# Decode attention and MLP: the projection of 24 heads is placed between score pieces, and one V multiplication is cut into portions

## The chip, the cores and the metric

The kernel runs on one core of a Trainium2 chip. The metric is the device time of one execution in microseconds (us), the median of several runs. Profiled numbers come from one execution recorded by the hardware profiler. In the profile PE is TensorE (PEld its weight loads), DVE is VectorE, ACT is ScalarE, POOL is GpSimd, and SP is SyncE, which here does nothing but issue DMAs.

## The reference

One decode step of a pre-norm transformer block with a KV cache: 4 sequences (B), one new token each (Sq = 1), width D = 640, 32 heads of 128, 4096 cached keys, and an MLP of width F = 1728 with the Mish activation. All inputs are bfloat16.

```
ln = layernorm(x)
q  = (ln @ wq)                          # 4 x 32 heads x 128
s  = q . k_cache * Dh**-0.5             # per sequence and head: 4096 scores
o  = softmax(s) @ v_cache
h  = x + o.reshape(B, Sq, H*Dh) @ wo
m  = layernorm(h) @ w1 + b1
h2 = h + (m * tanh(softplus(m))) @ w2   # output
```

Each of the K and V caches is 4 x 32 x 4096 x 128 bfloat16, 134 MB. Every element of them is read once.

## The kernel before

**Octets.** The 128 pairs of sequence and head are worked off in 16 groups of 8, called octets here (`NU = 16`). In an octet each pair owns 16 partitions, each partition holds 256 keys (`R = 256`), and K and V of an octet are 8 MB each. The first 14 octets (`NL`) go through one loop on PE (L631); the last two, `U = 14` (the last but one) and `L = 15` (the last), are written out after the loop. They hold the last head rows of two sequences each.

**Scores.** K comes in two halves, `kt[0]` and `kt[1]`, of 128 keys per partition (`RK = 128`), 4 MB each. DVE multiplies K by q in place, a quarter-half at a time (`dve_scores`, L508), four products for a half. PE sums each product over a part of the head width by 8 matmuls against an identity held in the array; such a block of 8 is a *piece* (`pe_pieces`, L428 to L444), and an octet has 8 of them. Each piece waits for its product on the semaphore `to_pe`. Two pieces fill one of two PSUM banks, which DVE then reduces to scores (L494).

**Softmax.** `softmax` (DVE, ACT) and `pe_softmax` (PE) work together: DVE takes row maxima, PE turns them by a small matmul (`tr_row`), DVE reduces, PE spreads the result (`nb_ps`), ACT takes the exponential, DVE masks the weights into a tile `e` of 8 columns per key (L555), and PE sums the rows (`l_ps`). For octet L, `e2[1]` is laid into `kt[1]`, whose scores are done by then.

**V.** `pv_moving` (L464) multiplies rows of V with `e`, four keys per matmul, V moving, into one PSUM bank `p_ps`: 64 matmuls for an octet. ACT copies the bank out (`act_copy`), PE adds its blocks into `ot_b` (`add_blocks`), DVE divides by the sums (`normalise`). There is one V buffer, `v_sb`.

**Projection.** `regroup` turns the normalised outputs of up to six groups of 4 heads into `o4` (PE, then a copy by ACT); `project(hq)` (L658) multiplies one group of 4 heads by `wo`: 20 matmuls of 4 columns, accumulated in `yT_b`. There are 8 such groups (`HQ`); the first 6 (`QA`, 24 heads) are complete after the loop.

**Load queue.** All big loads are issued in program order by SP, each behind explicit waits (`after(sp, ...)`) that protect the buffer it overwrites; one late wait holds back all loads behind it. After the loop the order is: the first half of U's V (L679); the first half of L's K, behind U's fourth piece (L697); the second half of L's K, behind U's last piece (L699); the second half of U's V (L701); the first half of L's V, behind the multiplication of the first half of U's V (L707); the second half of L's V in three steps of a quarter, an eighth and an eighth, behind the multiplication of the second half of U's V (L716); then w1 and w2 into `kt[0]` (L725 to L733).

**PE's order after the loop.** `regroup` of the 24 heads; 14 small matmuls that turn the bias b1, which DVE copies to `b1T` (L688, L689); `project` of the six groups (L691); the pieces of U, its softmax matmuls; V rows 0 to 128 of U (`pv_a`, L706); the pieces of L, its softmax matmuls; V rows 128 to 256 of U (`pv_b`, L714); U's `add_blocks`; V rows 0 to 128 of L; `regroup` and `project` of the seventh group; V rows 128 to 192 of L, then `add_blocks`, then rows 192 to 256 straight into `ot_b` (L754); the eighth group's projection; second layernorm and MLP. The waits on PE, DVE and ACT are all written out by hand, and each engine works strictly in program order.

Of the kernel before, what the change touches and what calls it, by code (L numbers as in the profile page):

```python
# [30 lines left out]
def kernel(  # L31
# [31 lines left out]
    te, ve, ac, po, sp = nc.tensor, nc.vector, nc.scalar, nc.gpsimd, nc.sync  # L63
# [8 lines left out]
    R = Sk // PH  # L72
    KT = 2
    RK = R // KT
# [9 lines left out]
    NL = NU - 2  # L84
# [8 lines left out]
    C2 = F // 128  # L93
    FREM = F - C2 * 128
    FC = C2 + 1
    W1_PARTS = ((0, 3), (3, DC))
    QA = HQ - 2
# [3 lines left out]
    def sb(name, shape, dtype=FP32):  # L101
# [15 lines left out]
    b1_row = sb("b1_row", [1, F], BF16)  # L117
    ident = sb("ident", [128, 128], BF16)
# [17 lines left out]
    e2 = [  # L136
        sb("e2_0", [128, R, R8], BF16)[:, :, :],
        kt[1][:, :, :].rearrange("p r d -> p (r d)")[:, 0 : R * R8].rearrange("p (r i) -> p r i", i=R8),
    ]
# [5 lines left out]
    rs8 = sb("rs8", [128, R8])  # L145
# [4 lines left out]
    b1T = sb("b1T", [128, FC])  # L150
# [5 lines left out]
    s_b = [bank("s0"), bank("s1")]  # L156
# [6 lines left out]
    y2_b = bank("y2_b")  # L163


    pe = Events(tc, "pe")
    dve = Events(tc, "dve")
# [16 lines left out]
    def after(engine, *events):  # L184
        for sem, n in events:
            if seen.get((engine.engine, id(sem)), 0) < n:
                seen[engine.engine, id(sem)] = n
                engine.wait_ge(sem, n)
# [5 lines left out]
    def take(sem, k=1):  # L194
        te.wait_ge(sem, k)
        te.sem_inc(sem, -k)  # L196

    def mm(out_, lhsT, rhs, start=True, stop=True):
        return te.matmul(out_, lhsT=lhsT, rhs=rhs, start=start, stop=stop)  # L199
# [41 lines left out]
    k_ready, v_ready = {}, {}  # L241
# [22 lines left out]
    def load_v(u, r0=0, r1=R):  # L264
        for part, view in keys_in(u, A_v_cache, r0, r1):
            dma = sp.dma_start(out=v_sb[part, r0:r1, :], in_=view)
            if u < NL:
                dma.then_inc(v_in, 16)
            else:
                name = f"v{u}_{r0}"  # L270
                if name not in loads:
                    loads[name] = Events(tc, name)
                v_ready[u, r0] = loads[name].by(dma, 16)
# [8 lines left out]
            out=ident[:, :],  # L282
            in_=ident[:, :],
# [23 lines left out]
    for s in range(n_sub):  # L307
# [11 lines left out]
            out=ln1[:, :],  # L319
# [13 lines left out]
    for src, dst in ((ln1_v, tp[0]), (x_v, tp[1])):  # L333
        for c in range(DC):
            i = mm(dst[:, c, :], src[:, c, :], ident[0:N, 0:N])
# [7 lines left out]
    for b in range(N):  # L343
        ve.tensor_copy(
            out=sel_o[:, b, :, :],
            in_=id32[:, b, :].unsqueeze(2).to_broadcast([N * R8, R8, PH]),
        )
    for k in range(NB):
        ev = ve.tensor_copy(
            out=sel_b[:, k, :, :, :],  # L350
            in_=ident[0 : N * R8, 0 : N * R8]
# [6 lines left out]
    with nc.allow_low_precision("ones and zeros"):  # L358
        ve.tensor_reduce(
            out=mask[0][:, :],  # L360
            in_=ident[:, :].rearrange("p (i x) -> p i x", i=R8),
# [4 lines left out]
            out=mask[1][:, :].rearrange("p (b q) -> p b q", b=NB),  # L366
            in_=ident[:, :].rearrange("p (q x b) -> p b q x", q=G, b=NB),
# [5 lines left out]
            out=pick[:, :],  # L373
            in_=ident_f[:, :].rearrange("p (t i) -> p i t", t=T),
# [42 lines left out]
    for k in range(NB):  # L417
        i = mm(
            qb[:, k, :],
            sel_b[:, k, :, :, :].rearrange("r q x b -> r (q x b)"),  # L420
            q_st[:, HO - 1, :],
        )
# [2 lines left out]
    qb_ok[N] = act.by(ac.copy(out=qbs[:, NL:NU, :], in_=qb))  # L425


    def pe_pieces():  # L428
        te.ldweights(ident[:, :])
        done = []  # L430
        for k in range(KT):
            for part in range(NP):
                for j in range(NQ):
                    take(to_pe.sem)
                    for d in range(j * DQ, (j + 1) * DQ, W):
                        i = mm_held(
                            s_ps[part],
                            ident[:, :],
                            kt[k][:, part * RP : (part + 1) * RP, d : d + W],
                            start=(d == 0),  # L440
                            stop=(d == Dh - W),
                        )
                    done.append(pe.by(i))
        return done  # L444

    tr_row = small[0:1, 0:128]
# [1 line left out]
    l_ps = small[:, 136 : 136 + R8]  # L448
    ot_ps = [ot_b[:, i * R8 : (i + 1) * R8] for i in range(2)]

    def pe_softmax():
        done = []
        for o, lhsT, rhs in (
            (tr_row, pm, ident_f),
            (nb_ps, nscale, mx),
            (l_ps, ones_f, rs8),
        ):
            take(to_pe.sem)
            done.append(pe.by(mm(o, lhsT[:, :], rhs[:, :])))

        take(to_pe.sem)
        return done

    def pv_moving(e, r0, r1, last):  # L464
        for r in range(r0, r1, J):
            c0 = 128 // T * (r // J % T)
            i = mm(
                p_ps[c0 : c0 + J * R8, :],
                e[:, r : r + J, :].rearrange("p j i -> p (j i)"),
                v_sb[:, r : r + J, :].rearrange("p j d -> p (j d)"),  # L470
                start=(r < J * T),
                stop=(r >= last - J * T),
            )
        return i
# [44 lines left out]
    def softmax(u, done, e):  # L519
        to_pe.by(ve.tensor_reduce(out=pm[:, :], in_=s_sb[:, :], axis=AX.X, op=ALU.max))  # L520
        after(ve, done[0])
        if rows(u) is None:
            m = mask[0]
            o, i = mx[:, :], tr_row.rearrange("o (i x) -> o i x", i=R8)
        else:
            m = mask[1]
            o = mx[:, :].rearrange("o (b q) -> o b q", b=NB)
            i = tr_row.rearrange("o (q x b) -> o b q x", q=G, b=NB)
        to_pe.by(ve.tensor_reduce(out=o, in_=i, axis=AX.X, op=ALU.max))  # L529

        after(ve, done[1])
        then(ve, dve, ve.tensor_tensor(out=nb8[:, :], in0=nb_ps, in1=m[:, :], op=ALU.mult))  # L532
        after(ac, dve.by(ve.tensor_reduce(out=nbs[:, :], in_=nb8[:, :], axis=AX.X, op=ALU.add)))  # L533
        exp_ok = act.by(
            ac.activation(  # L535
                out=e1[:, :],
                in_=s_sb[:, :],
                func=ACT.Exp,
                bias=nbs[:, :],
                scale=SCALE,  # L540
                accum_out=rs[:, u : u + 1],
            )
        )

        after(ve, exp_ok)
        to_pe.by(
            ve.tensor_tensor(  # L547
                out=rs8[:, :],
                in0=rs[:, u : u + 1].to_broadcast([128, R8]),
                in1=m[:, :],  # L550
                op=ALU.mult,
            )
        )
        to_pe.by(
            ve.tensor_tensor(  # L555
                out=e,
                in0=e1[:, :].unsqueeze(2).to_broadcast([128, R, R8]),
                in1=m[:, :].unsqueeze(1).to_broadcast([128, R, R8]),
                op=ALU.mult,
            )  # L560
        )
        after(ve, done[2])
        return dve.by(ve.reciprocal(out=rl[u % 2][:, :], in_=l_ps))

    def act_copy(done):
        after(ac, done)
        p_out.by(ac.copy(out=p_sb[:, :], in_=p_ps[:, :]))  # L567
# [29 lines left out]
    wo_in = b1_in = None  # L597
    wo = Events(tc, "ld_wo")
    for u in range(NL):
# [6 lines left out]
        if N <= u < 2 * N:  # L606

            after(sp, all_q)
            for h in range(2 * (u - N) * G, 2 * (u - N + 1) * G, G):
# [4 lines left out]
                        out=wo_sb[:, h : h + G, :],  # L614
                        in_=A_wo[h * Dh : (h + G) * Dh, :].rearrange(order, i=G),
# [55 lines left out]
    def f_chunk(rows, c):  # L671

        if c < CK * CI:
            k, i = divmod(c, CI)
            block = rows[:, k * 128 * CI : (k + 1) * 128 * CI]
            return block.rearrange("p (f i) -> p i f", i=CI)[:, i, :], 128
        return rows[:, c * 128 : min(F, (c + 1) * 128)], min(F - c * 128, 128)

    load_v(NL, 0, RK)  # L679
    after(te, otn_ok)  # L680
    o4_ok = regroup(0, QA)
    after(te, b1_in)
    b_ps = s_b[0][:, 0:FC]
    for c in range(FC):
        cols, fw = f_chunk(b1_row[:, :], c)
        i = mm(b_ps[0:fw, c : c + 1], cols, ident[0:1, 0:1])
    after(ve, pe.by(i))
    ve.tensor_copy(out=b1T[:, 0:C2], in_=b_ps[:, 0:C2])  # L688
    ve.tensor_copy(out=b1T[0:FREM, C2:FC], in_=b_ps[0:FREM, C2:FC])  # L689
    after(te, o4_ok, wo_in)  # L690
    for hq in range(QA):  # L691
        project(hq)


    U, L = NL, NL + 1
    done_u = pe_pieces()
    after(sp, done_u[NP * NQ - 1])  # L697
    load_k(KT * L)
    after(sp, done_u[-1])  # L699
# [1 line left out]
    load_v(U, RK, R)  # L701
    dve_scores(U, done_u)
    done_s = pe_softmax()
    softmax(U, done_s, e2[0])
    after(te, v_ready[U, 0])
    pv_a = pe.by(pv_moving(e2[0], 0, RK, R))  # L706
    after(sp, pv_a)  # L707
    load_v(L, 0, RK)
    done_l = pe_pieces()
    dve_scores(L, done_l)  # L710
    done_s = pe_softmax()
    after(ve, softmax(L, done_s, e2[1]))
    after(te, v_ready[U, RK])
    pv_b = pe.by(pv_moving(e2[0], RK, R, R))  # L714
    act_copy(pv_b)
    after(sp, pv_b)  # L716
    V_LAST = (RK, R - R // 4, R - R // 8, R)
    for r0, r1 in zip(V_LAST, V_LAST[1:]):
        load_v(L, r0, r1)


# [22 lines left out]
    o4_ok = regroup(QA, QA + 1)  # L744
# [210 lines left out]
```

## Time and profile before

| | |
|---|---|
| median of 3 runs | 676.8 us (674.76 to 677.09) |
| the profiled execution | 674.94 us |
| its span, first to last instruction | 673.1 us |
| granted TensorE clock, mean | 0.816 of full |
| busy: PE, DVE, ACT | 422.3, 390.6, 28.4 us |
| moved from memory | 283.35 MB, 421 GB/s over the span |

The span is what the profile covers; the time of an execution is a little longer. A timeline row has start, length (us), engine, line, operation, output and inputs, shape and count, and in brackets the idle time of the engine before it and what ended it. Almost all PE rows carry L199, the helper `mm`; they are told apart by their tiles. A DMA issue row says when SP issued the load; its landing is told by the DMA table.

### The profile page before, as it was taken

How to read it: one execution, taken by the hardware profiler on the slowest of the kernel's cores; microseconds unless marked ns; L12 is line 12 of the kernel's file. 1: busy time of each engine (PE TensorE's matmuls, PEld its weight loads, DVE VectorE, ACT ScalarE, POOL GpSimd, SP SyncE). 2: the span in 40 equal slices, each digit the busy share in tenths (PEclk: the TensorE clock that was granted, in tenths of full speed). 3: DMA queues.
4: the chain of work that ended last, by engine and by line, in shares of the span. 5: the costliest groups of instructions: out<-in, count | busy, mean ns of one | idle time of the engine just before them, and what ended most of it. 6: DMA issues, size and time to landing. Idle time of an engine off the chain costs nothing. (4 is left out here: it accounts for less than half of the span.)

```text
span 673.1 us, 5296 instructions
## 1 busy us (share of the span) xinstructions
PE 422.3 (63%) x2727; PEld 85.9 (13%) x1719; DVE 390.6 (58%) x362; ACT 28.4 (4%) x65; POOL 0.8 (0%) x7
## 2 busy tenths in 40 slices
PE   0785767576575655746656466656748665776656
PEld 0202010010202011020110201102020100401025
DVE  2292946748492854818548185674828477477712
ACT  0200000000000000000000000000000000000011
POOL 0000000000000000000000000000000000000000
PEclk9897787969697786968879778796978779697975
DMA  9999999999999999999999999999999999999966
GB/s 372 436 439 430 443 421 448 415 458 432 409 463 407 461 401 432 440 430 450 421 446 438 411 442 426 442 423 428 454 411 458 411 462 411 434 415 394 415 249 268
DMA packets 11011, 283.50 MB, mean 421 GB/s; under 512 B 1331, under 2 KB 2039, under 8 KB 4088
## 3 DMA queue, kind: packets, MB, share of 16 engines
q1 hardware_dynamic: 10992, 283.36, 98.1%
q8 instruction: 6, 0.10, 0.1%
q14 instruction: 5, 0.04, 0.0%
q10 hardware_dynamic: 8, 0.01, 0.0%
HBM read 283.35 MB, written 0.01 MB: 421 GB/s over the span
## 5 line engine op out<-in xcount | busy, mean ns | idle before, releaser
L203 PE MATMUL s<-kt,ident 128*128 128x512 bf16 x1024 | 267.4, 414 | 125.4 <-PEq L196 125.4
L508 DVE TENSOR_TENSOR kt<-kt,qbs 128x4096 bf16<-128x4096 bf16 x128 | 287.0, 2283 | 49.7 <-DMA kt<-in_A_k_cache_dram 26.4
L199 PE MATMUL p_ps<-v_sb,e 128*32 128x512 bf16 x960 | 89.0, 550 | 31.8 <-PEq L196 31.8
L579 DVE TENSOR_TENSOR otn<-ot_b,rl 128x8 bf16<-128x8 f32 x16 | 2.7, 167 | 131.5 <-PE ot_b L199 131.5
L494 DVE TENSOR_REDUCE s_sb<-s 128x64 f32<-128x512 f32 x64 | 44.0, 687 | 58.0 <-PE s L203 58.0
L199 PEld LDWEIGHTS small<-ident_f,pm 128*1 128x1 f32 x32 | 1.8, 80 | 412.2 <-issue 412.2
L199 PEld LDWEIGHTS p_ps<-v_sb,e 128*32 128x32 bf16 x960 | 36.6, 131 | 77.3 <-issue 72.4
L555 DVE TENSOR_TENSOR e<-e,mask 128x2048 bf16<-128x2048 bf16 x15 | 34.3, 2284 | 0.0
L535 ACT ACTIVATE e<-s_sb,nbs 128x256 bf16<-128x256 f32 x16 | 8.1, 507 | 465.1 <-DVE nbs L533 465.1
L199 PE MATMUL ot_b<-pick,p_sb 128*128 128x8 f32 x128 | 17.3, 262 | 12.5 <-PEq L196 12.5
L199 PE MATMUL small<-rs,ones_f 128*128 128x8 f32 x32 | 7.2, 297 | 22.1 <-PEq L196 22.1
L199 PE MATMUL small<-ident_f,pm 128*1 128x128 f32 x32 | 6.1, 270 | 21.3 <-PEq L196 21.3
L199 PEld LDWEIGHTS ot_b<-pick,p_sb 128*128 128x128 f32 x128 | 16.3, 199 | 20.4 <-issue 20.4
L199 PE MATMUL h_b<-w_sb,xz 128*32 128x512 bf16 x40 | 10.3, 425 | 11.3 <-DMA w_sb<-in_A_wq_dram 11.3
L567 ACT COPY p_sb<-p_ps 128x512 f32<-128x512 f32 x16 | 9.4, 586 | 134.6 <-PE p_ps L199 134.6
L199 PE MATMUL small<-mx,nscale 1*128 1x8 f32 x32 | 5.8, 252 | 7.4 <-PEq L196 7.4
L529 DVE TENSOR_REDUCE mx<-small 1x8 f32<-1x128 f32 x16 | 4.5, 278 | 9.1 <-PE small L199 9.1
L199 PEld LDWEIGHTS small<-rs,ones_f 128*128 128x128 f32 x32 | 6.2, 240 | 23.1 <-issue 23.1
L547 DVE TENSOR_TENSOR rs<-rs,mask 128x8 f32<-128x8 f32 x16 | 2.7, 167 | 10.7 <-ACT e L535 10.7
L532 DVE TENSOR_TENSOR nb<-small,mask 128x8 f32<-128x8 f32 x16 | 2.7, 167 | 8.8 <-PE small L199 8.8
L520 DVE TENSOR_REDUCE pm<-s_sb 128x1 f32<-128x256 f32 x16 | 6.7, 420 | 0.5
L199 PEld LDWEIGHTS h_b<-w_sb,xz 128*32 128x32 bf16 x40 | 4.2, 107 | 17.0 <-DMA w_sb<-in_A_wq_dram 11.4
(99 smaller groups left out, 75.2 us busy)
## 6 DMA issues: line engine op xcount, KB each, us to landing
kt<-in_A_k_cache_dram SPq DMA_DIRECT2D x28, 4096.0 KB, 25.6
kt<-in_A_k_cache_dram SPq DMA_DIRECT2D x6, 2048.0 KB, 21.1
v_sb<-in_A_v_cache_dram SPq DMA_DIRECT2D x6, 2048.0 KB, 20.5
w_sb<-in_A_wq_dram SPq DMA_DIRECT2D x1, 5120.0 KB, 15.4
w_sb<-in_A_wo_dram SPq DMA_DIRECT2D x8, 640.0 KB, 36.6
kt<-in_A_k_cache_dram SPq DMA_DIRECT2D x4, 1024.0 KB, 10.7
v_sb<-in_A_v_cache_dram SPq DMA_DIRECT2D x2, 1024.0 KB, 6.5
v_sb<-in_A_v_cache_dram SPq DMA_DIRECT2D x4, 512.0 KB, 9.4
```

The costliest lines, as they stand in the source:

```text
L199: return te.matmul(out_, lhsT=lhsT, rhs=rhs, start=start, stop=stop)
L203: return te.add_instruction(mybir.InstMatmult(name=nc.get_next_instruction_name(), engine=PE, ins=[te.lower_ap(rhs), te.lower_ap(lhsT, for ...
L494: return ve.tensor_reduce(out=s_sb[:, n * RP : (n + 1) * RP], in_=s_ps[n % NP], axis=AX.X, op=ALU.add,)
L508: ve.tensor_tensor(out=piece, in0=piece, in1=qbs[:, u, j * DQ : (j + 1) * DQ].unsqueeze(1).to_broadcast([128, RP, DQ]), op=ALU.mult,)
L520: to_pe.by(ve.tensor_reduce(out=pm[:, :], in_=s_sb[:, :], axis=AX.X, op=ALU.max))
L529: to_pe.by(ve.tensor_reduce(out=o, in_=i, axis=AX.X, op=ALU.max))
L532: then(ve, dve, ve.tensor_tensor(out=nb8[:, :], in0=nb_ps, in1=m[:, :], op=ALU.mult))
L535: ac.activation(out=e1[:, :], in_=s_sb[:, :], func=ACT.Exp, bias=nbs[:, :], scale=SCALE, accum_out=rs[:, u : u + 1],)
L547: ve.tensor_tensor(out=rs8[:, :], in0=rs[:, u : u + 1].to_broadcast([128, R8]), in1=m[:, :], op=ALU.mult,)
L555: ve.tensor_tensor(out=e, in0=e1[:, :].unsqueeze(2).to_broadcast([128, R, R8]), in1=m[:, :].unsqueeze(1).to_broadcast([128, R, R8]), op=AL ...
L567: p_out.by(ac.copy(out=p_sb[:, :], in_=p_ps[:, :]))
L579: ve.tensor_tensor(out=o, in0=ot_ps[max(u - NL, 0)].rearrange("p (h q) -> p h q", **shape), in1=rl[u % 2][:, :].rearrange("p (h q) -> p h ...
```

## The change

The order of work after PE's loop is changed in three places; what is computed stays.

- `pe_pieces` takes a list of functions, `between`. After piece i it calls the i-th function and loads the identity into the array again. The six groups of the 24-head projection are given to U's pieces in this way, one behind each of the first six, instead of all ahead of them. The 14 matmuls that turn b1 move behind U's softmax matmuls; their target moves to the end of the bank `y2_b`, and DVE's two copies move behind U's softmax.
- The multiplication of the first half of U's V is split: 16 matmuls ahead of L's pieces and four portions of 4 matmuls behind each of L's first four pieces. The load of the first half of L's V waits for the last portion.
- The multiplication of the second half of U's V moves from behind L's softmax matmuls: rows 128 to 192 directly behind L's pieces, rows 192 to 256 between the second and third softmax matmul (`pe_softmax` takes a function for that place). The load of the third quarter of L's V waits for the first of these, the loads of the last two eighths for the second. ACT copies the bank after the second.

```diff
-    def pe_pieces():
+    def pe_pieces(between=()):
         te.ldweights(ident[:, :])
...
                     done.append(pe.by(i))
+                    if len(done) <= len(between):
+                        between[len(done) - 1]()
+                        te.ldweights(ident[:, :])
...
-    def pe_softmax():
+    def pe_softmax(between=None):
...
+            if rhs is rs8 and between is not None:
+                between()
             take(to_pe.sem)
             done.append(pe.by(mm(o, lhsT[:, :], rhs[:, :])))
...
     o4_ok = regroup(0, QA)
-    after(te, b1_in)
-    b_ps = s_b[0][:, 0:FC]
-    for c in range(FC):
-        cols, fw = f_chunk(b1_row[:, :], c)
-        i = mm(b_ps[0:fw, c : c + 1], cols, ident[0:1, 0:1])
-    after(ve, pe.by(i))
-    ve.tensor_copy(out=b1T[:, 0:C2], in_=b_ps[:, 0:C2])
-    ve.tensor_copy(out=b1T[0:FREM, C2:FC], in_=b_ps[0:FREM, C2:FC])
-    after(te, o4_ok, wo_in)
-    for hq in range(QA):
+    b_ps = y2_b[:, 512 - FC : 512]
+
+    def project_first(hq):
+        after(te, o4_ok, wo_in)
         project(hq)
+    def turn_b1():
+        after(te, b1_in)
+        for c in range(FC):
+            cols, fw = f_chunk(b1_row[:, :], c)
+            i = mm(b_ps[0:fw, c : c + 1], cols, ident[0:1, 0:1])
+        return pe.by(i)
-    done_u = pe_pieces()
+    done_u = pe_pieces([lambda hq=hq: project_first(hq) for hq in range(QA)])
     after(sp, done_u[NP * NQ - 1])
     load_k(KT * L)
...
     done_s = pe_softmax()
-    softmax(U, done_s, e2[0])
+    b1_ok = turn_b1()
+    after(ve, softmax(U, done_s, e2[0]))
+    after(ve, b1_ok)
+    ve.tensor_copy(out=b1T[:, 0:C2], in_=b_ps[:, 0:C2])
+    dve.by(ve.tensor_copy(out=b1T[0:FREM, C2:FC], in_=b_ps[0:FREM, C2:FC]))
     after(te, v_ready[U, 0])
-    pv_a = pe.by(pv_moving(e2[0], 0, RK, R))
-    after(sp, pv_a)
+    VA = RK // 8
+    pv_moving(e2[0], 0, RK // 2, R)
+    pv_a = []
+    def pv_some(i):
+        r0 = RK // 2 + i * VA
+        pv_a.append(pe.by(pv_moving(e2[0], r0, r0 + VA, R)))
+    done_l = pe_pieces([lambda i=i: pv_some(i) for i in range(4)])
+    after(sp, pv_a[-1])
     load_v(L, 0, RK)
-    done_l = pe_pieces()
     dve_scores(L, done_l)
-    done_s = pe_softmax()
+    after(te, v_ready[U, RK])
+    R_MID = R - R // 4
+    pv_b = [pe.by(pv_moving(e2[0], RK, R_MID, R))]
+    done_s = pe_softmax(lambda: pv_b.append(pe.by(pv_moving(e2[0], R_MID, R, R))))
     after(ve, softmax(L, done_s, e2[1]))
-    after(te, v_ready[U, RK])
-    pv_b = pe.by(pv_moving(e2[0], RK, R, R))
-    act_copy(pv_b)
-    after(sp, pv_b)
+    act_copy(pv_b[1])
     for r0, r1 in zip(V_LAST, V_LAST[1:]):
+        after(sp, pv_b[r0 > RK])
         load_v(L, r0, r1)
```

More of the change, by code (lines that the diff above doesn't have):

```diff
@@ L679 @@
     load_v(NL, 0, RK)
+    U, L = NL, NL + 1
     after(te, otn_ok)
     o4_ok = regroup(0, QA)
-    after(te, b1_in)
-    b_ps = s_b[0][:, 0:FC]
-    for c in range(FC):
-        cols, fw = f_chunk(b1_row[:, :], c)
-        i = mm(b_ps[0:fw, c : c + 1], cols, ident[0:1, 0:1])
-    after(ve, pe.by(i))
-    ve.tensor_copy(out=b1T[:, 0:C2], in_=b_ps[:, 0:C2])
-    ve.tensor_copy(out=b1T[0:FREM, C2:FC], in_=b_ps[0:FREM, C2:FC])
-    after(te, o4_ok, wo_in)
-    for hq in range(QA):
-        project(hq)
-    U, L = NL, NL + 1
-    done_u = pe_pieces()
+    b_ps = y2_b[:, 512 - FC : 512]
+    def project_first(hq):
+        after(te, o4_ok, wo_in)
+        project(hq)
+    def turn_b1():
[5 more added lines that the diff above has]
+    done_u = pe_pieces([lambda hq=hq: project_first(hq) for hq in range(QA)])
     after(sp, done_u[NP * NQ - 1])
```

## The prediction, made before the changed kernel was run

> **What bounds the kernel now.** I read the page's busy times, slices and DMA queues first.
>
> ```profile
> PE 422.3 (63%) x2727; PEld 85.9 (13%) x1719; DVE 390.6 (58%) x362; ACT 28.4 (4%) x65; POOL 0.8 (0%) x7
> DMA packets 11011, 283.50 MB, mean 421 GB/s; under 512 B 1331, under 2 KB 2039, under 8 KB 4088
> q1 hardware_dynamic: 10992, 283.36, 98.1%
> ```
>
> 283 MB pass at 421 GB/s and the one load queue fills 98.1% of the span, while no compute engine is busy above 63%. So the time is the bytes at that rate, plus the stretches in which the DMA engines have nothing to move. The busy time by stretches finds them (columns: stretch, its length, busy us and count of PE, PEld, DVE, ACT, POOL, then granted clock, DMA share, GB/s):
>
> ```profile
> 608.00:612.00 4.00, 1.14 (x6) 0.79 (x4) 2.50 (x5) 0.60 (x2) 0.00 (x0) 0.75 0.83 254
> 616.00:636.00 20.00, 15.24 (x68) 0.10 (x1) 16.96 (x12) 0.00 (x0) 0.00 (x0) 0.98 1.03 442
> 638.00:640.00 2.00, 0.57 (x2) 0.50 (x2) 1.33 (x3) 0.60 (x2) 0.00 (x0) 0.50 0.46 197
> 640.00:645.00 5.00, 3.25 (x32) 1.24 (x32) 1.32 (x2) 0.36 (x1) 0.00 (x0) 0.59 0.00 0
> 645.00:647.00 2.00, 1.63 (x23) 1.31 (x27) 0.17 (x1) 0.23 (x1) 0.00 (x0) 1.00 0.57 131
> 647.00:667.00 20.00, 12.09 (x242) 9.56 (x234) 2.68 (x15) 4.24 (x8) 0.00 (x0) 0.60 1.01 413
> 667.00:673.00 6.00, 2.61 (x71) 2.27 (x71) 0.94 (x5) 0.00 (x0) 0.00 (x0) 0.50 0.09 26
> ```
>
> From 638 to 647 there is a hole: nothing moves for five microseconds, and little around them. Against 421 GB/s the rows lack (421-197) x 2 + 421 x 5 + (421-131) x 2 = 3130 KB, which is **7.4 us**. A second dip at 608 to 612 lacks (421-254) x 4 = 668 KB, **1.6 us**. The rows of 20 us (442 and 413) lack little; at 667 the work runs out. Why the hole is there, the timeline of the load queue (SP) and of PE shows, and the table of SP's waits from 590 on (us in total, times, longest):
>
> ```profile
> 606.54 3.07 SPq L255 DMA_DIRECT2D kt<-in_A_k_cache_dram  x4
> 616.26 1.11 SPq L266 DMA_DIRECT2D v_sb<-in_A_v_cache_dram  x2
> 644.64 3.71 SPq L266 DMA_DIRECT2D v_sb<-in_A_v_cache_dram  x6
> 648.79 5.96 SPq L180 DMA_DIRECT2D kt<-in_B_w_dram  x6
> 641.35 3.25 PE L199 MATMUL p_ps<-v_sb,e 128*32 128x512 bf16 x32 [1.63 <-PEq L196]
> ```
>
> ```profile
> SPq L266 <- PE p_ps L199: 32.3, 2, 27.2
> ```
>
> After 616.26 the next load is issued at 644.64, 0.04 us after the second half of the last V but one is multiplied (641.35 + 3.25); that wait was 27.2 us. The queue drained at about 639. What came late is the last V's second half (4 MB in three steps, six loads) and w1, w2 behind it. What follows on PE hangs on their landing (first the DMA table: KB each, median us to landing; then the timeline):
>
> ```profile
> v_sb<-in_A_v_cache_dram SPq DMA_DIRECT2D x2, 1024.0 KB, 6.5
> w2s_sb<-in_B_w_dram SPq DMA_DIRECT2D x1, 160.0 KB, 13.2
> ```
>
> ```profile
> 646.33 1.91 PE L199 MATMUL p_ps<-v_sb,kt 128*32 128x512 bf16 x32
> 648.70 0.65 PE L199 MATMUL yT_b<-o,w_sb 128*128 128x4 bf16 x20 [0.30 <-ACT o L654]
> 653.25 1.90 PE L199 MATMUL p_ps<-v_sb,kt 128*32 128x512 bf16 x16 [3.90 <-DMA v_sb<-in_A_v_cache_dram]
> 669.14 0.29 PE L199 MATMUL y_b<-act_t,w2s_sb 128*128 128x4 bf16 x5
> ```
>
> PE has multiplied the last V's first half and projected at 649.35, then waits 3.90 us for the third quarter: its two loads land 6.5 us after issue in the median, the later one by 653.25. From there to the span's end are 19.85 us, which run through work that waits on data a second time: w2s, the last load, issued some 7.0 us after 648.79, lands 13.2 us later, at 669.0, and its matmuls run from 669.14. So the end stands within 0.2 us of the load stream, whatever the chain of waits says of the engines in between.
>
> **The change part by part.** Three edits.
>
> *The loads of the last V's second half* wait no longer for the whole multiplication. It is cut in two: 16 matmuls directly behind the last scores, 16 between the second and third small matmul of the softmax. The first cut releases the third quarter's loads, the second the rest. The rows around the last scores:
>
> ```profile
> 633.12 1.89 PE L203 MATMUL s<-kt,ident 128*128 128x512 bf16 x8 [0.91 <-PEq L196]
> 636.34 0.43 PE L199 MATMUL small<-ident_f,pm 128*1 128x128 f32 x2 [1.33 <-PEq L196]
> 637.24 0.53 PE L199 MATMUL small<-mx,nscale 1*128 1x8 f32 x2 [0.46 <-PEq L196]
> 638.92 2.28 DVE L555 TENSOR_TENSOR kt<-e,mask 128x2048 bf16<-128x2048 bf16 x1
> 639.15 0.57 PE L199 MATMUL small<-rs,ones_f 128*128 128x8 f32 x2 [1.38 <-PEq L196]
> ```
>
> Scores end at 635.01. 16 matmuls at 1.91/32 = 0.06 us each (granted clock 1.00) are 0.96; with 0.25 allowed for the start they end at 636.2, just inside the wait before 636.34; at 3.25/32 = 0.10 each (clock 0.50) they would delay the softmax by 0.5. The second 16 start at 637.77 and end by 638.7 to 639.4; the third small matmul then starts up to 0.3 after its 639.15, and DVE needs it only after its 2.28 us at 641.20: hidden. If that cover went, it would cost those 0.3. So the first two loads are issued at 636.3 instead of 644.64, the other four at 639.5, when the queue still holds the third quarter (2.1 MB, 5.0 us). The hole closes: **-7.4**. The dip at 608 goes with the next edit, so far as the loads issued at 606.54 come earlier: 0 to -1.6, I take the middle, **-0.8**. The load stream is then 8.2 earlier; w1 and w2 move with it, being behind it in the same queue.
>
> *The loads of the last V's first half*, issued at 616.26 behind the multiplication of 32, now come behind 16 matmuls and four portions, the last after the fourth piece: about 612.5 + 4 x 6.64/3 + 0.7 (a reduction) + 1.9 (a piece) + 0.4 (a portion) = 624.4. Behind this wait on SP stand the last V's second half, w1 and w2. The queue needs the loads when what precedes them is drained: 4.2 MB are 10.0 us and it ended at about 639, so at 629. Spare 4.6 us: cost **0**; with the spare gone, one for one.
>
> *The projection of 24 heads* (120 matmuls) leaves its place ahead of the scores of the last octet but one, and its six groups go between the pieces:
>
> ```profile
> 579.90 0.71 PE L199 MATMUL s<-ident,b_row 1*128 1x1 bf16 x14
> 580.65 0.17 DVE L688 COPY b1T<-s 128x13 f32<-128x13 f32 x1 [1.09 <-PE s L199]
> 580.54 3.02 PE L199 MATMUL yT_b<-o,w_sb 128*128 128x4 bf16 x107
> 586.14 0.51 PE L199 MATMUL yT_b<-o,w_sb 128*128 128x4 bf16 x13 [2.59 <-issue]
> 586.51 6.80 PE L203 MATMUL s<-kt,ident 128*128 128x512 bf16 x24
> 612.51 6.64 DVE L508 TENSOR_TENSOR kt<-kt,qbs 128x4096 bf16<-128x4096 bf16 x3
> 591.62 0.69 DVE L494 TENSOR_REDUCE s_sb<-s 128x64 f32<-128x512 f32 x1 [4.14 <-PE s L203]
> 550.04 0.69 DVE L494 TENSOR_REDUCE s_sb<-s 128x64 f32<-128x512 f32 x1 [1.42 <-PE s L203]
> 596.83 1.89 PE L203 MATMUL s<-kt,ident 128*128 128x512 bf16 x8 [0.31 <-PEq L196]
> 599.62 1.89 PE L203 MATMUL s<-kt,ident 128*128 128x512 bf16 x8 [0.91 <-PEq L196]
> ```
>
> PE spent 580.54 to 586.65 on it, 2.59 of this idle; DVE, its first products ready, waited 4.14 us for the first scores where the octet before waited 1.42. That difference, 2.7, goes. DVE also starts without the wait for b1 and its two copies (1.09, and 0.3 together), 0 to 1.2 earlier, according to when its K has landed; I take 0.3. Added are six groups of 20 x 3.02/107 = 0.56 and a reload of the identity of at most 0.1 (14 matmuls with their weight loads took 0.71, 0.05 each): 0.66 a group. The gaps between pieces are 0.31 and 0.91, so a pair of groups (1.32) has 1.22 of cover; the first group stands before the first half-tile's second piece with no cover, 0.7. This octet ends 2.7 + 0.3 - 0.7 = 2.3 earlier (0 to 3.9). The b1 step comes back behind its softmax: 14 matmuls, 0.71, a hand-over of 0.1 and the copies, 0.3: DVE waits for PE there, with the copies and the last octet's first product queued behind the wait, and starts that octet 1.1 later than it could. The four portions of V (4 x 0.06 to 0.10, and 0.1) lie in the gaps of 0.31 and 0.91. Last octet: **1.2 earlier** (1 later to 2.5 earlier).
>
> *What is late next on PE.* DVE's weights are ready at 641.20 - 1.2 = 640.0. Then the blocks are added and the last V's first half is multiplied at once, where before the earlier V was multiplied first. The blocks' 8 matmuls, and the landing of the two loads issued at 616.26:
>
> ```profile
> 645.37 1.03 PE L199 MATMUL ot_b<-pick,p_sb 128*128 128x8 f32 x8 [0.78 <-PEq L196]
> ```
>
> ```profile
> DMA to landing us min/median/max: 20.0/22.1/24.3
> ```
>
> So 0.15 + 1.03, then 32 matmuls at 1.91 or 3.25, then 1.11 from their end to the end of the projection (648.24 to 649.35). Their V half is no obstacle: issued by 616.8, it landed up to 24.3 us later, at 641.1, and now 0.8 earlier. (The earlier V's second half, for which PE now waits ahead of the softmax, is 4.2 MB ahead of it in the queue, so landed by 631.1.) Before the change PE came to the 32 matmuls out of others and with the clock at 1.00 (row 645 to 647). Now it comes out of a pause of nearly 2 us, as it came to those at 641.35, in a row with a mean clock of 0.59; so I take that row's 3.25, with 1.91 as the other end: 640.0 + 0.15 + 1.03 + 3.25 + 1.11 = 645.5.
>
> The Trainium skill, "TensorE: Matmul & The Clock Gate", Part 1, has the array fall to half clock after an idle window of some 3.4 us and come back after as much sustained work, which speaks against the change at this place: the matmuls that used to warm PE are gone. The two rows agree with it; by the rule this step is the slow one and PE is ready at 645.5, without it at 644.2.
>
> *The sum.* The third quarter lands at 653.25 - 8.2 = 645.0; PE is ready at 645.5. So it starts 653.25 - 645.5 = 7.7 earlier, and w2s, 8.2 earlier, does not hold up the end. The span becomes 673.1 - 7.7 = 665.4, the profiled execution's 674.94 (1.84 more than its span) becomes 667.2. That execution lies near the low end of the three runs (674.76 to 677.09, median 676.8); from the median it would be 669.1. I say **668.2**, between the two.
>
> **Rivals.** *PE takes the place of the loads.* The octets end no earlier or 1 later, because the inserted groups keep PE from its full clock. Then PE is ready 1.2 to 2.2 later, at 646.7 to 647.7, and the gain is 6.5 to 5.5: 668.4 to 669.4 by the profiled run, up to 671.3 by the median. For it: the first 24 score matmuls behind the projection took 6.80, 0.28 each, against 1.89/8 = 0.24 later. Against it: pieces with gaps of up to 0.91 between them ran at a mean clock of 0.98 (616 to 636).
>
> *Slower: PE is not fed its instructions.* The 2.59 us idle at 586.14 lies inside 120 matmuls with no wait in the code. If every one of the six insertions met such a stall, the octet would end 15.5 - 2.3 = 13.2 later, the loads of 606.54 with it, and the queue, dry at about 608, would lose about that; less the 7.4 closed, the time is 674.9 + 5.8 = 681. It decides from 7.4 + 2.3 = 9.7 us, 1.6 per insertion. Against it: the row stands alone, none of the others quoted has such an idle that ends in "issue".
>
> The page "Runtime: NRT & Kernel Launch" of the Trainium skill, Instruction fetch mechanics, says that instructions are fetched in blocks ahead of use, mostly hidden, and that a taken branch breaks this; the trace's one stall follows shortly after PE's loop ends, which would fit once and not six times.
>
> *The hole only moves.* Should the first half of the last V be issued after 629 rather than at 624.4, a new gap opens; with the last octet 12 us late (4.6 + 7.4) it would equal the old one: about 675, no gain. Only the stalls above could do this.
>
> **How the numbers follow.** Forecast 0.72; PE as the bound 0.15; a hole that moves 0.05; starved PE 0.08. Range: the best case is 7.4 + 1.6 = 9.0 with PE ready in time, 665.9, and one microsecond for the spread of runs: 664.8. The worst inside is the first rival from the median and a further 0.9 for a softmax that is delayed twice: 672.3. Outside lie the last two rivals, 0.13. Half a per cent, 3.4 us, is about what a measurement of this kernel tells from no change. Faster 0.87 (the first two), same 0.05, slower 0.08.
>
> **What would show it.** Right: the DMA share stays near 1 from 608 to about 659; the third quarter's loads are issued within 1.5 us of the last piece; the wait at the third quarter shrinks from 3.90 to under 1; DVE's wait for the first scores of the last octet but one is about 2. Wrong: idle PE inside the inserted groups, the loads of 616.26 issued after the queue has drained, or the same 20 us behind the third quarter becoming longer because w1 or w2 lands late.

## The result, and the profile after

The changed kernel takes 666.8 us (median of 6 runs, 666.5 to 668.9), the kernel before 675.7 us in the same series (674.7 to 677.1): a ratio of 0.987, 95% interval 0.985 to 0.989. The profiled execution took 666.89 us with a span of 665.0, against 674.94 and 673.1.

First the busy time by stretches of the changed kernel, in the columns used above:

```profile
608.00:612.00 4.00, 2.36 (x28) 1.49 (x32) 3.17 (x5) 0.00 (x0) 0.00 (x0) 0.50 0.98 418
616.00:636.00 20.00, 16.95 (x92) 1.23 (x38) 15.79 (x11) 0.00 (x0) 0.00 (x0) 0.95 1.03 442
636.00:638.00 2.00, 1.54 (x20) 0.65 (x19) 0.61 (x3) 0.43 (x2) 0.00 (x0) 1.00 0.69 246
638.00:640.00 2.00, 0.47 (x6) 0.30 (x2) 1.79 (x2) 0.75 (x3) 0.00 (x0) 1.00 0.96 410
640.00:645.00 5.00, 4.13 (x40) 2.27 (x41) 0.86 (x3) 0.00 (x0) 0.00 (x0) 0.70 1.00 416
647.00:658.00 11.00, 8.33 (x176) 7.46 (x173) 1.77 (x10) 4.07 (x7) 0.00 (x0) 0.58 1.02 412
658.00:665.00 7.00, 2.48 (x71) 2.18 (x71) 1.84 (x8) 0.00 (x0) 0.00 (x0) 0.50 0.11 34
```

The last two columns answer the rows of before. From 638 to 645 the load stream runs at 410 and 416 GB/s where there were 197 and 0, and at 608 to 612 it runs at 418 where there were 254. One dip is left, 636 to 638 at 246: (421-246) x 2 = 350 KB, 0.8 us. So of the hole's 7.4 us 6.6 are gone and of the second dip all 1.6: 8.2, against 8.1 by which the span is shorter.

The load queue of the changed kernel:

```profile
604.07 2.39 SPq L255 DMA_DIRECT2D kt<-in_A_k_cache_dram  x4
624.98 1.11 SPq L266 DMA_DIRECT2D v_sb<-in_A_v_cache_dram  x2
635.64 4.92 SPq L266 DMA_DIRECT2D v_sb<-in_A_v_cache_dram  x6
640.99 5.30 SPq L180 DMA_DIRECT2D kt<-in_B_w_dram  x6
```

The last V's second half is released at 635.64 instead of 644.64, its first half at 624.98 instead of 616.26. On PE and DVE:

```profile
583.19 3.57 PE L203 MATMUL s<-kt,ident 128*128 128x512 bf16 x8 [2.27 <-PEq L196]
586.55 0.72 PE L199 MATMUL yT_b<-o,w_sb 128*128 128x4 bf16 x20
589.14 0.69 DVE L501 TENSOR_REDUCE s_sb<-s 128x64 f32<-128x512 f32 x1 [1.67 <-PE s L203]
613.49 3.57 PE L203 MATMUL s<-kt,ident 128*128 128x512 bf16 x8 [0.82 <-PEq L196]
619.71 0.69 DVE L501 TENSOR_REDUCE s_sb<-s 128x64 f32<-128x512 f32 x1 [1.94 <-PE s L203]
634.65 0.69 DVE L501 TENSOR_REDUCE s_sb<-s 128x64 f32<-128x512 f32 x1 [2.04 <-PE s L203]
641.83 3.54 PE L199 MATMUL p_ps<-v_sb,kt 128*32 128x512 bf16 x32
646.39 1.19 PE L199 MATMUL p_ps<-v_sb,kt 128*32 128x512 bf16 x16
648.35 1.46 PE L199 MATMUL ot_b<-pick,p_sb 128*128 128x8 f32 x8 [0.78 <-PEq L196]
```

DVE waits 1.67 us for the first scores of the last octet but one (before 4.14), but 1.94 for those of the last (620.12 in the trace before: 0.96). The last scores are reduced at 634.65, 0.4 earlier than before (635.05). The 32 matmuls of the last V's first half take 3.54, and the third quarter is multiplied at 646.39 with no wait ahead of it.

### The profile page after: what moved, and what is told of

It is laid out like the page before. It is cut to its first block, busy times and chain, and to the rows that moved or that the text cites. A ratio compares the mean times of both kernels' runs of the same rounds, so it can differ in the third digit from the quotient of the medians.

```text
span 665.0 us, 5307 instructions
## 1 busy us (share of the span) xinstructions
PE 423.2 (64%) x2727; PEld 86.0 (13%) x1729; DVE 390.6 (59%) x362; ACT 28.4 (4%) x65; POOL 0.8 (0%) x7
## 5 line engine op out<-in xcount | busy, mean ns | idle before, releaser
L203 PE MATMUL s<-kt,ident 128*128 128x512 bf16 x1024 | 270.2, 417 | 125.3 <-PEq L196 125.3
L199 PE MATMUL p_ps<-v_sb,e 128*32 128x512 bf16 x960 | 88.0, 541 | 28.5 <-PEq L196 28.5
```

What stands on the lines that cost most here:

```text
L203: return te.add_instruction(mybir.InstMatmult(name=nc.get_next_instruction_name(), engine=PE, ins=[te.lower_ap(rhs), te.lower_ap(lhsT, for ...
```

## The experiments

Each is compared with the kernel before in runs on the same chip; the changed kernel stands at 0.9871 (0.9853 to 0.989) in a series of its own. The diffs are against the changed kernel, and "..." marks lines left out. The theory is that the time is the load stream's, and that the gain is the hole closed by releasing the last V's second half early. Its rivals are that the earlier scores bring it, or PE's order at the end.

### One edit alone

The first kernel has only the split multiplication of the earlier V's second half; projection, b1 and first half are those of before:

```diff
-    done_u = pe_pieces([lambda hq=hq: project_first(hq) for hq in range(QA)])
+    (b1 turned and copied, project_first(hq) for all six groups)
+    done_u = pe_pieces()
...
-    pv_moving(e2[0], 0, RK // 2, R)
-    done_l = pe_pieces([lambda i=i: pv_some(i) for i in range(4)])
-    after(sp, pv_a[-1])
+    pv_a = pe.by(pv_moving(e2[0], 0, RK, R))
+    after(sp, pv_a)
     load_v(L, 0, RK)
+    done_l = pe_pieces()
```

> Only the split of the second half of the last V but one, with the early release of the last V's second half; projection, b1 and the first half as before. Theory 'hole' (the time is the load stream's, and the gain is the gap closed near 640): 6 to 7 us of the 8.9 remain, ratio 0.989 to 0.992, no stretch without loads after 636, the dip near 608 still there. Rival 'scores' (the gain is that the scores of the last two octets come earlier): at most 2 us, ratio 0.997 or more.

Measured: 668.5 us, ratio 0.990 (0.989 to 0.992), span 664.4. In the load queue the second half of the last K and the release, and the stretch at 608:

```profile
605.16 2.39 SPq L255 DMA_DIRECT2D kt<-in_A_k_cache_dram  x4
634.62 4.92 SPq L266 DMA_DIRECT2D v_sb<-in_A_v_cache_dram  x6
```

```profile
608.00:612.00 4.00, 1.33 (x10) 0.85 (x14) 3.33 (x5) 0.60 (x2) 0.00 (x0) 0.56 0.96 410
```

As the theory had it, except that the dip at 608 is small here too (410 GB/s): this execution issued the loads of the last K's second half at 605.16, 1.4 earlier than before. It is also the fastest of its five (666.2 to 669.8 us); whether the dip is larger in the slower ones, no trace shows.

The second has only the interleaved projection and the moved b1. The first half of the earlier V is whole again here too (not shown), and its second half stands behind the softmax matmuls:

```diff
...
-    pv_b = [pe.by(pv_moving(e2[0], RK, R_MID, R))]
-    done_s = pe_softmax(lambda: pv_b.append(pe.by(pv_moving(e2[0], R_MID, R, R))))
+    done_s = pe_softmax()
     after(ve, softmax(L, done_s, e2[1]))
+    pv_b = [pe.by(pv_moving(e2[0], RK, R, R))] * 2
```

> Only the six projection groups between the pieces, and b1 behind the softmax; both V multiplications as before. Theory 'hole': the loads of the last V's second half still wait for all 32 matmuls, so the gap near 640 stays, shorter by what the last octet ends earlier: 1 to 2 us gained, ratio 0.997 to 0.9985. Rival 'scores': 5 us or more, ratio 0.993 or less.

Measured: 672.9 us, ratio 0.996 (0.9945 to 0.9974), 1.8 to 3.7 us of gain: somewhat over what the theory gave, well under the rival's 5. The release comes 1.6 earlier and the hole is still there; the profiled span, 671.6, is 1.5 shorter:

```profile
643.06 3.71 SPq L266 DMA_DIRECT2D v_sb<-in_A_v_cache_dram  x6
```

```profile
636.00:644.00 8.00, 4.20 (x37) 1.99 (x37) 2.81 (x5) 1.19 (x3) 0.00 (x0) 0.59 0.08 33
```

### The hole opened again, with all else changed

```diff
     act_copy(pv_b[1])
     V_LAST = (RK, R - R // 4, R - R // 8, R)
+    add_u = pe.by(add_blocks(ot_ps[0]))
+    after(sp, add_u)
     for r0, r1 in zip(V_LAST, V_LAST[1:]):
-        after(sp, pv_b[r0 > RK])
         load_v(L, r0, r1)
...
-    add_u = pe.by(add_blocks(ot_ps[0]))
```

> The changed kernel with every engine's order of compute, but the loads of the last V's second half released only when PE has added the blocks of the octet before, near 642. Theory 'hole': a gap of 4 to 6 us opens again and the time rises by 4 to 5.5 us, to 671 to 672.5 (ratio 0.993 to 0.995). Rival 'scores' or 'order on PE': the time stays within 1 us of the changed kernel, ratio 0.986 to 0.989.

Measured: 672.7 us, ratio 0.9956 (0.9942 to 0.997), span 670.0: time and ratio lie a little above the theory's 671 to 672.5 and 0.993 to 0.995, far from the rivals'. In the load queue, by stretches, and on PE:

```profile
641.49 3.80 SPq L266 DMA_DIRECT2D v_sb<-in_A_v_cache_dram  x6
```

```profile
638.00:642.00 4.00, 1.99 (x18) 1.60 (x22) 2.36 (x3) 0.26 (x1) 0.00 (x0) 0.90 0.03 12
```

```profile
645.34 0.65 PE L199 MATMUL yT_b<-o,w_sb 128*128 128x4 bf16 x20 [0.30 <-ACT o L661]
649.05 1.90 PE L199 MATMUL p_ps<-v_sb,kt 128*32 128x512 bf16 x16 [3.06 <-DMA v_sb<-in_A_v_cache_dram]
```

PE has projected at 645.99, as early as in the changed kernel (646.47), and then waits 3.06 us for the load. The release is 5.85 later and the span 5.0 longer. PE's order is that of the changed kernel, and nothing else was altered: this shows the cause.

### The first half's portions undone

```diff
-    pv_moving(e2[0], 0, RK // 2, R)
-    done_l = pe_pieces([lambda i=i: pv_some(i) for i in range(4)])
-    after(sp, pv_a[-1])
+    pv_a = pe.by(pv_moving(e2[0], 0, RK, R))
+    after(sp, pv_a)
     load_v(L, 0, RK)
+    done_l = pe_pieces()
```

> The changed kernel with the first half of the last V but one multiplied whole ahead of the last octet's pieces, as before, and the load behind it issued some 9 us earlier. Theory 'hole': that load was early enough either way, so only PE's later start of the last octet counts: 0 to 1 us slower, ratio 0.987 to 0.9885. Rival: the portions are what lets the stream run through; then 2 us or more slower. Other rival: the earlier load closes what is left of the dip near 637, 0.5 us faster.

Measured: 666.2 us, ratio 0.9869 (0.9849 to 0.9889): no difference from the changed kernel. Behind it stands something that I had not expected:

```profile
613.80 5.63 PE L203 MATMUL s<-kt,ident 128*128 128x512 bf16 x24
632.40 0.69 DVE L501 TENSOR_REDUCE s_sb<-s 128x64 f32<-128x512 f32 x1 [2.04 <-PE s L203]
645.03 1.05 PE L199 MATMUL p_ps<-v_sb,kt 128*32 128x512 bf16 x16
649.46 1.01 PE L199 MATMUL ot_b<-kt,v_sb 128*128 128x8 bf16 x32 [0.69 <-DMA v_sb<-in_A_v_cache_dram]
659.79 0.42 PE L199 MATMUL y_b<-act_t,kt 128*128 128x4 bf16 x10 [0.21 <-DMA kt<-in_B_w_dram]
```

32 matmuls ahead of the pieces bring PE's clock back, the first 24 score matmuls follow in 5.63, and the last scores are reduced at 632.40. That is 28.7 us after the last scores of the octet before (603.72), where the changed kernel needs 30.6 (604.08 to 634.65): the portions cost the last octet 1.9 us. PE begins the third quarter 1.36 earlier, and then waits 0.69 for the last eighth of V and 0.21 for w2; the span is 664.4. So the load stream takes most of the gain on PE back. The loads of the first half, issued some 10 us earlier, did not close the dip either: 287 GB/s from 636 to 638.

### PE kept at its clock

```diff
             done.append(pe.by(mm(o, lhsT[:, :], rhs[:, :])))
+        for _ in range(warm_mm):               # 8, for the last octet only
+            mm(s_b[0][:, :], ident[:, :], w_sb[:, 0:512])
         take(to_pe.sem)
```

> The changed kernel with 8 matmuls added that feed nothing (identity by 512 columns of wo, into a free bank), placed on PE in its pause between the last octet's third softmax matmul and its weights. Theory 'clock' (the 32 matmuls of the last V's first half take 3.25 to 3.6 us because PE comes out of a pause at half clock): they take about 1.9, PE stands before the third quarter 1.5 us earlier and waits there for the load; and since the load stream is close behind, the time gains only 0 to 0.6 us, ratio 0.986 to 0.988. Rival 'PE bounds the end': 1.5 us faster, ratio 0.985 or less. Rival 'no clock effect': the 32 matmuls stay at 3.25 or more.

Measured: 668.0 us, ratio 0.9886 (0.9867 to 0.9905), not faster, and a little above the theory's 0.986 to 0.988.

```profile
638.38 1.67 PE L199 MATMUL s<-w_sb,ident 128*128 128x512 bf16 x7
641.26 1.91 PE L199 MATMUL p_ps<-v_sb,kt 128*32 128x512 bf16 x32
643.62 0.65 PE L199 MATMUL yT_b<-o,w_sb 128*128 128x4 bf16 x20 [0.30 <-ACT o L663]
646.12 1.05 PE L199 MATMUL p_ps<-v_sb,kt 128*32 128x512 bf16 x16 [1.84 <-issue]
```

```profile
644.54 0.09 PEld L199 LDWEIGHTS p_ps<-v_sb,kt 128*32 128x32 bf16 x1 [0.35 <-DMA v_sb<-in_A_v_cache_dram]
```

Behind the idle matmuls (7 of the 8 are in the records) the 32 take 1.91: that is the clock. PE has projected at 644.27, 2.2 earlier than in the changed kernel, and a row of its weight loads shows the third quarter's load awaited until 644.54. Then PE stands idle to 646.12 with nothing to wait for ("issue"), so that it begins about when the changed kernel does. The DMA view of that stretch, 643.5 to 646.2, has one packet on a queue of its own (columns: packets, MB, share of the 16 engines' time):

```profile
q8 instruction: 1, 0.02, 2.2%
```

So the clock is worth 1.6 us on these 32 matmuls, and here it was lost again, to a fetch of instructions as it seems (more on this below). Which of the two, PE or the load stream, bounds the end, this run does not tell.

### Released earlier still

Two portions of 8 matmuls behind the last octet's sixth and seventh piece take the place of the 16 behind its last:

```diff
-    pv_b = [pe.by(pv_moving(e2[0], RK, R_MID, R))]
...
+    # pv_more(i), not printed: wait for V, 8 matmuls; pv_b[0] is the event of the second
-    done_l = pe_pieces([lambda i=i: pv_some(i) for i in range(4)])
+    done_l = pe_pieces(
+        [lambda i=i: pv_some(i) for i in range(4)]
+        + [lambda: None]
+        + [lambda i=i: pv_more(i) for i in range(2)]
+    )
```

> The changed kernel with the first 16 matmuls of the earlier V's second half put into two portions behind the last octet's sixth and seventh piece, so that the third quarter's loads are issued near 633 instead of 635.6. Theory 'late release' (the dip in the load rate near 637 is what is left of the gap): the dip goes, 0.5 to 0.9 us faster. Rival 'the stream's own unevenness': the dip stays where one load follows another, time within 0.4 us of the changed kernel.

Measured: 668.9 us, ratio 0.9893 (0.9875 to 0.9911), not faster: neither of the two times came.

```profile
633.77 7.97 SPq L266 DMA_DIRECT2D v_sb<-in_A_v_cache_dram  x6
```

```profile
636.00:638.00 2.00, 0.41 (x3) 0.17 (x3) 1.23 (x3) 0.00 (x0) 0.00 (x0) 1.00 0.68 295
```

```profile
642.06 1.84 PE L199 MATMUL ot_b<-pick,p_sb 128*128 128x8 f32 x8 [1.99 <-PEq L196]
648.33 1.05 PE L199 MATMUL p_ps<-v_sb,kt 128*32 128x512 bf16 x16
```

The release is 1.9 earlier and the dip is still there (295 GB/s): it is not a late release. The last scores came 1.2 later than in the changed kernel (635.84; 0.4 of it within the last octet, the rest ahead of what was edited), the blocks were added in 1.84 where it was 1.03, and PE came to the third quarter at 648.33, 1.9 later, with no wait. The span, 667.0, is 2.0 longer. Here PE is the bound, as the first rival of the prediction had it.

The next kernel takes all that makes PE early at once: the first half whole, these two portions, and the 8 idle matmuls.

> The first half of the earlier V multiplied whole again, the first 16 matmuls of its second half behind the sixth and seventh piece, and the 8 idle matmuls: every step that makes PE ready earlier at the third quarter, at once. Theory 'the load stream bounds the end': PE is ready 2 to 3 us earlier and waits for the load; the time is within 0.7 us of the changed kernel, ratio 0.986 to 0.988. Rival 'PE bounds the end': 2 us or more faster, ratio 0.984 or less.

Measured: 666.7 us, ratio 0.9867 (0.9846 to 0.9889), span 664.4, no difference from the changed kernel. PE was not early, for two reasons. The first portion waits for the earlier V's second half, and pieces seven and eight with it:

```profile
630.04 0.61 PE L199 MATMUL p_ps<-v_sb,e 128*32 128x512 bf16 x8 [1.88 <-DMA v_sb<-in_A_v_cache_dram]
```

So the last scores came 30.7 us after those of the octet before (604.18 to 634.90), where the kernel with the first half whole needs 28.7. And the idle matmuls ran at half clock (2.94 us for 7) and were in PE's way. The third quarter began at 646.18, where the changed kernel has 646.39, so this run says nothing of an early PE either.

### PE early at the third quarter

Another kernel has the first half whole and the 8 idle matmuls under one weight load, 9 instructions for 16:

```diff
+        te.ldweights(ident[:, :])
+        for _ in range(8):                     # for the last octet only
+            mm_held(s_b[0][:, :], ident[:, :], w_sb[:, 0:512], True, True)
         take(to_pe.sem)
```

> The first half of the last V is multiplied whole ahead of the last octet's pieces, and behind the last scores PE runs 8 matmuls of 512 columns that nothing uses, with one weight load for all of them, so 9 instructions where the kernel with idle matmuls had 16. Both together are to bring PE to the third quarter with no fetch of instructions in its way: last scores at about 632.4 (as with the first half whole), 32 matmuls in 1.9, projected at about 641.5 to 643.3. Theory (the load stream bounds the end; PE is only near it): PE then waits at least 1 us for the third quarter's load or the last eighth's, which land where they did, the span is 664.0 to 665.0, and the ratio to the kernel before is 0.985 to 0.988, that of the changed kernel. Rival (PE bounds the end in the changed kernel, since it came to the third quarter 1.5 us after the load): the span falls by what PE comes earlier, 1.5 to 3 us, to 662 to 663.5, ratio 0.983 or less. If PE idles there again with nothing awaited, the run decides nothing.

Measured: 666.6 us, ratio 0.9859 (0.9836 to 0.9883), span 664.9, no difference from the changed kernel.

```profile
643.61 0.65 PE L199 MATMUL yT_b<-o,w_sb 128*128 128x4 bf16 x20 [0.30 <-ACT o L665]
644.71 0.61 PE L199 MATMUL p_ps<-v_sb,kt 128*32 128x512 bf16 x6 [0.44 <-DMA v_sb<-in_A_v_cache_dram]
646.12 0.90 PE L199 MATMUL p_ps<-v_sb,kt 128*32 128x512 bf16 x10 [0.81 <-issue]
649.50 1.85 PE L199 MATMUL ot_b<-kt,v_sb 128*128 128x8 bf16 x64
```

The last scores came at 634.07 and not at 632.4, but PE had projected at 644.26 all the same. It waits 0.44 for the load, less than the theory's 1 us, multiplies 6 of the 16, and idles 0.81 with nothing to wait for. The third quarter is done at 647.02 (changed kernel: 646.39 + 1.19 = 647.58), and the 64 matmuls behind it start only 0.17 earlier. The rival's 1.5 us did not come, though by the condition that I had set for it the run alone decides nothing.

What decides is the last load, w2s, in the changed kernel: its issue and its matmuls in the timeline, its landing in the table of DMA issues:

```profile
647.43 0.98 SPq L180 DMA_DIRECT2D w2s_sb<-in_B_w_dram  x1
661.04 0.29 PE L199 MATMUL y_b<-act_t,w2s_sb 128*128 128x4 bf16 x5
```

```profile
w2s_sb<-in_B_w_dram SPq DMA_DIRECT2D x1, 160.0 KB, 13.1
```

It lands at 647.43 + 13.1 = 660.5, and its matmuls start at 661.04. However early PE is, the end comes at most 0.5 earlier while the loads stand where they do. With the first half whole PE did wait for w2 (the row at 659.79 above), and the span was 0.6 shorter. In all three kernels with a span of 664.4 w2s lands 0.1 us ahead of its matmuls (at 660.3 to 660.4 by its issue and the DMA table), so there a faster PE could bring the end at most 0.1 earlier. In the kernel with portions behind pieces six and seven, where PE is late, it lands 2.4 ahead.

### The idle time inside the projection

One more kernel is the changed one with the projection back in its old place, b1 staying behind the softmax:

```diff
-    done_u = pe_pieces([lambda hq=hq: project_first(hq) for hq in range(QA)])
+    for hq in range(QA):
+        project_first(hq)
+    done_u = pe_pieces()
```

> The changed kernel with the six projection groups back ahead of the scores, b1 staying behind the softmax, to look at the idle time inside the projection. Theory 'instruction supply by count': 14 matmuls fewer stand ahead of it, so the idle time of 2.2 to 2.6 us moves 14 matmuls further, to the end of the projection or into the first piece. Rival 'bound to the projection' (a bank, the wo tile): it stays behind the 107th matmul. Time 1 to 2.5 us above the changed kernel either way.

Measured: 669.4 us (one run), 2.6 above the changed kernel, span 667.6.

```profile
580.13 0.34 PE L199 MATMUL y_b<-otn,ident 128*32 128x24 bf16 x16 [0.68 <-DVE otn L586]
580.87 3.36 PE L199 MATMUL yT_b<-o,w_sb 128*128 128x4 bf16 x120 [0.39 <-ACT o L661]
586.14 7.32 PE L203 MATMUL s<-kt,ident 128*128 128x512 bf16 x24 [1.91 <-issue]
```

```profile
608.00:612.00 4.00, 1.22 (x6) 0.79 (x6) 2.35 (x5) 0.60 (x2) 0.00 (x0) 0.83 0.83 250
```

All 120 matmuls now run through, and the idle time, 1.91, stands behind them, ahead of the first piece. So no tile is to blame. A count of PE's records (matmuls, weight loads and semaphore instructions together) from the regrouping on gives a rule that fits: the idle time stands behind 275 of them in the kernel before, here, and in the one with the split V alone. In the two kernels whose idle matmuls ran at full clock it stands behind 786, 511 later. In the kernel before, the DMA view of 583.5 to 584.6, where that idle time begins, has the packet of instructions too:

```profile
q8 instruction: 1, 0.02, 5.0%
```

It starts at 583.65, and PE goes on 2.5 later. In all five kernels PE goes on 2.2 to 2.5 us after the start of such a packet. The changed kernel goes on behind record 787 at 646.96, 2.35 after its packet (644.61), and its weight loads idle for only 0.25: PE came there later, its 32 matmuls having run at half clock. Its record 275 falls between the pieces of the octet, at 596.48, and the packet for it, at 591.00, cost nothing. So the interleaving did remove the idle 2.59 us of the kernel before. The dip at 608 is back here (250 GB/s).

### All releases together

| kernel | third quarter released | span | from release to end |
|---|---|---|---|
| before | 644.64 | 673.1 | 28.5 |
| projection alone | 643.06 | 671.6 | 28.5 |
| hole opened again | 641.49 | 670.0 | 28.5 |
| projection in its old place | 638.37 | 667.6 | 29.2 |
| changed | 635.64 | 665.0 | 29.4 |
| idle matmuls | 635.06 | 665.0 | 29.9 |
| first half whole, idle matmuls | 635.05 | 664.9 | 29.9 |
| split V alone | 634.62 | 664.4 | 29.8 |
| portions behind pieces six and seven | 633.77 | 667.0 | 33.2 |
| first half whole | 633.38 | 664.4 | 31.0 |
| all at once | 633.08 | 664.4 | 31.3 |

Down to 641.5 the span follows the release one for one; at 638.4 0.7 of it is lost. Below 636 the span stops at 664.4 to 665.0: no gap is left in the stream but the dip at 636, and an earlier release did not close it. The one exception is the kernel in which PE is late. Release and span of a row come from one execution; the median times of the split V alone and of the idle matmuls lie 2.3 and 1.2 us above it, so those two rows are good cases.

## Why the prediction was right, step by step

- **The hole** was the cause, shown by opening it again. I counted 7.4; 6.6 went. What is left at 636 to 638 stays when the release is earlier; what makes it stays open.
- **The dip at 608**, of which I took the half, 0.8, went whole, 1.6: a term that was sized too small. It is there in the two profiles that issue the second half of the last K at 606.5 to 606.7 (254 and 250 GB/s), and not in those that issue it by 605.2 (401 to 430). That is a comparison between kernels that differ in more, no experiment on the dip alone.
- **The first half in portions** costs no time, as forecast, and was issued at 624.98 where I had 624.4. But it was not free on PE: 1.9 us on the last octet's scores, hidden by the stream but for at most 0.6 of the span.
- **The projection** ended the octet 2.5 earlier (last piece 604.04 against 606.51; forecast 2.3). The b1 step cost its 1.1: DVE began the last octet 1.4 earlier (611.10 against 612.51). But the gain at that octet's end was 0.4 and not 1.2: behind 16 matmuls instead of 32, PE was at half clock, its first piece took 3.57, and DVE waited 1.94 where 0.96 had been. This step of mine failed. I had put the portions into gaps that only exist at full clock.
- **PE at the third quarter**: forecast 645.5 with 3.25 for the 32 matmuls, measured 646.39 with 3.54. The load, forecast for 645.0, was issued at 635.64 and 636.16; its later half landed 8.6 after its issue, at 644.8, so PE was the later by 1.6.
- **From there to the end** I took over the 19.85 of before; it became 18.6, since PE came to the third quarter out of other matmuls: 1.19 against 1.90, and 1.46 against 1.85 for adding the blocks. This made up for the 0.9 by which PE was late, and that was luck. The span of 665.0 against 665.4 is closer than the steps deserve. That w2s ends within 0.2 us of its use held roughly: 0.5.
- **The first rival**, PE as the bound, is half true: in the changed kernel the end could come 0.5 earlier for a faster PE, and a PE 1.9 later at the third quarter makes the span 2.0 longer (portions behind pieces six and seven).
- **Starved PE** did not come as I had drawn it, once per insertion: the widest idle time ahead of a piece between the groups is 0.41. The chance of 0.08 was small for the right reason, but my cause, the loop's end, was too narrow. The Trainium skill, "Runtime: NRT & Kernel Launch", Instruction fetch mechanics, has blocks of 16 KiB, 256 instructions, and the step of 511 records agrees. It calls the fetch mostly hidden; here 0.8 to 2.6 us stood bare where PE came to the end of a block less than 2.2 us after the packet's start, or ahead of it.
- **The median** fell by 8.9, the profiled execution by 8.05; of that difference I can only say that it lies in the spread of the runs before. By its own terms the range of the prediction is 664.9 to 672.2, a tenth off at each end; nothing hangs on it.

## What to carry to other kernels

Where one load queue holds the time, look for the stretch in which it moves nothing, find the issue that ends it, and see what that issue waits for; splitting the work behind which it waits gains the stretch, and no more. A release stops paying when it comes before the queue is empty, which a table of release times against spans shows at once. Before putting work into gaps of PE, ask at which clock those gaps were measured, and after taking idle time out of one engine, look at when the last load lands: that is all that the change can bring.

## What the runs showed of the hardware

PE's clock was decided by less than I had thought. 8 idle matmuls of 512 columns, 1.67 us of records, were enough to keep it up through a pause, and 32 matmuls of V then took 1.91 instead of 3.54. In the kernel with all at once the idle matmuls themselves ran at half clock (2.94 us), and the 32 behind them still took 1.91. Runs of narrow matmuls did not bring it back. Behind the last V, with 4 columns to a matmul, the clock of the changed kernel is at half, in the second row with PE busy all the time:

```profile
652.00:654.00 2.00, 1.24 (x23) 1.06 (x20) 0.75 (x5) 0.00 (x0) 0.00 (x0) 0.50 1.03 414
654.00:656.00 2.00, 2.00 (x47) 1.97 (x44) 0.42 (x3) 0.70 (x2) 0.00 (x0) 0.50 1.00 414
```

The Trainium skill, "TensorE: Matmul & The Clock Gate", Part 1, has the clock go by how busy PE was in a recent window of some 3.4 us. The pauses and the idle matmuls agree. Whether the narrow matmuls fail to count by their width or by the gaps on either side of the rows shown, no run here tells apart.
